# Loads of later chunks and of the check counted as landing later in the planner of a linear attention and MLP kernel

## The chip, the cores and the metric

The kernel runs on one core of a Trainium2 chip. The metric is device time in microseconds (us) of one execution. In the profile, PE is TensorE's matmul, PEld TensorE's weight load (which runs beside the matmuls), DVE is VectorE, ACT ScalarE, POOL GpSimd, SP SyncE, which here does nothing but issue DMAs.

## The reference

```python
# r, k, v, w: (4, 8, 768, 48); u: (8, 48)
for t in range(S):                                   # linear attention with decay
    kt, vt, rt, wt = (k[:, :, t], v[:, :, t], r[:, :, t], w[:, :, t])
    cur = np.einsum('bhd,bhe->bhde', u[None] * kt, vt)
    y[:, :, t] = np.einsum('bhd,bhde->bhe', rt, state + cur)
    state = wt[:, :, :, None] * state + np.einsum('bhd,bhe->bhde', kt, vt)
x = y.transpose(0, 2, 1, 3).reshape(3072, 384)
h = x @ w_in                                         # 384 -> 2048
g = np.maximum(h, 0.0) + alpha * np.minimum(h, 0.0)
out = g @ w_out                                      # 2048 -> 384
```

## The kernel before

**Chunks and groups.** The attention is cut into 24 chunks (q = 0 to 23) of 64 steps and two batches. Three chunks make a group of 384 tokens, and the eight groups go through the two matrix products of the MLP one after the other. A group's MLP is 16 units j, one for each 128 of the 2048 hidden features: `moe_up` (line 669: nine matmuls from x to a PSUM bank, in full and rest parts wh and wl), then the activation on ACT (line 674) and DVE (line 676), the split into gh (ACT, line 680) and its rest gl (DVE, line 681), and `moe_down` (line 694: three times three matmuls into op0, op1, op2). The products down of a unit follow those up by two units (`LAG`).

**A chunk's steps.** `load` issues its DMAs: wd (line 375), kr (line 376), rk (line 381, from chunk 5 on) and nv (line 382). `prep` works on them: two scans on DVE (lines 395 and 401) and two products into kr (lines 404 and 407), two products on POOL (line 425) that a reduction on DVE (line 428) makes cd of, and copies on ACT (line 433) into at. Then come a transpose of kr on PE (line 498) and a block of 128 small matmuls (line 452), which closes one chunk and opens the next; behind it stand x (ACT line 574, DVE line 585), the state St (DVE line 596) and the masked copies into at (line 483). When a group's third chunk is done, four small DMAs (line 606) move parts of x, and the group's units can begin. In each group from the third on, the second and the third chunk's blocks stand close together, about six microseconds apart; the text calls these two blocks a pair. There are pairs near 135, 193, 251, 311 and 371 us that other preparation follows.

**Weights and the check.** The 16 weight tiles are loaded (line 619) and unpacked on ACT (line 630) and DVE (lines 632, 635, 639: the product wf, one tile at a time), and split later into wh and wl (lines 650, 651). During the second half of the kernel, 12 pieces of wd and the 16 weight tiles are loaded a second time into two buffers raw (line 766) and tested on ACT (lines 774, 783, 784); the result is a flag that the end reads.

**What sets the order.** Nothing is ordered by hand. Every step is an `op` with an engine, a planned duration, a planned latency (`lat`) and a due time; `Plan.order` walks through a planned time and gives each free engine the ready step with the earliest due time. The instructions are then issued in that order, engine by engine, and on the chip every engine keeps to its order: an instruction whose input isn't there holds up all that stand behind it on its engine. For a load, the planned landing is in these lines:

```python
if e == "SP":
    dma = max(dma, end + DMA_LAT) + o.lat
    end = dma
```

with `DMA_LAT` 2.0 and 0.4 for the issue; the planned latencies are 1.5 for kr, 0.75 for wd and nv, 1.1 for rk and 2.0 for a piece of the check. `end` is when the steps that read the load become ready in the plan. The tiles come in rings: three for kr and nv, two for wd, rk and raw, so that the load of a chunk waits for the reader of the chunk two or three before it. Steps with `lock=True` on DVE and POOL aren't planned side by side.

## Time and profile before

| | |
|---|---|
| median of 3 runs | 511.61 us (507.61 to 512.86) |
| the profiled execution | 509.13 us, of which the profile's span is 507.3 us |
| PE busy, share of the span | 494.3 us, 97% |
| PEld busy | 457.8 us, 90% |
| DVE busy | 338.2 us, 67% |
| ACT busy | 290.8 us, 57% |
| mean granted clock of TensorE | 0.996 of full speed |

The profile is of one execution, which isn't one of the three runs. A matmul's row overlaps the next one's, so PE looks busy while it is short of work for a few tenths of a microsecond; the rows of PEld, one of which takes 0.19 us and which follow each other every 0.17 us when nothing is missing, show a wait at its full length.

### The profile page before, as it was taken

How to read it: one execution, taken by the hardware profiler on the slowest of the kernel's cores; microseconds unless marked ns; L12 is line 12 of the kernel's file. 1: busy time of each engine (PE TensorE's matmuls, PEld its weight loads, DVE VectorE, ACT ScalarE, POOL GpSimd, SP SyncE). 2: the span in 40 equal slices, each digit the busy share in tenths (PEclk: the TensorE clock that was granted, in tenths of full speed). 3: DMA queues.
4: the chain of work that ended last, by engine and by line, in shares of the span. 5: the costliest groups of instructions: out<-in, count | busy, mean ns of one | idle time of the engine just before them, and what ended most of it. 6: DMA issues, size and time to landing. Idle time of an engine off the chain costs nothing.

```text
span 507.3 us, 13038 instructions
## 1 busy us (share of the span) xinstructions
PE 494.3 (97%) x5404; PEld 457.8 (90%) x5404; DVE 338.2 (67%) x602; ACT 290.8 (57%) x746; POOL 79.4 (16%) x103
## 2 busy tenths in 40 slices
PE   8999998999999999999999999999999999999994
PEld 8976664699999999999998999989999999999994
DVE  7999999999886656938377474945566344343331
ACT  5866485453454536457584656667677676553331
POOL 2111333350114010402014020220000000000000
PEclk9999999999999999999999999999999999999998
DMA  8966776550352302735175653746455531210001
GB/s 311 365 212 228 265 238 213 151 161 23 111 149 79 112 22 77 221 90 202 49 216 163 159 175 105 237 131 205 147 179 159 170 127 63 88 42 6 1 3 53
DMA packets 27109, 72.42 MB, mean 143 GB/s; under 512 B 3680, under 2 KB 8224, under 8 KB 27040
## 3 DMA queue, kind: packets, MB, share of 16 engines
q1 hardware_dynamic: 26656, 71.19, 43.9%
q8 instruction: 44, 0.72, 0.6%
q10 hardware_dynamic: 384, 0.30, 0.2%
q14 instruction: 25, 0.20, 0.1%
HBM read 64.70 MB, written 4.72 MB: 137 GB/s over the span
## 4 chain that ended last, share of the span: by engine, by line
PE 78%; DVE 12%; DMA 5%; issue 2%; SPq 1%; ACT 1%; DVEq 0%; ACTq 0%
PE bank L669 35%; PE op L694 33%; PE bank L452 7%; DMA raw<-in_wts_dram 2%; DVE cx L635 2%; DVE wf L639 2%; DVE suf L395 2%; DMA kr<-in_dmaj_dram 1%; PE bank L498 1%; DVE pos L676 1%; DVE kr L404 1%; DVE kr L407 1%; DVE cx L632 1%; PE bank L561 1%; DVE wd L401 1%
## 5 line engine op out<-in xcount | busy, mean ns | idle before, releaser
L669 PE MATMUL bank<-x,wh 128*128 128x384 f32 x672 | 191.7, 339 | 0.5 <-DMA x<-x 0.5
L674 ACT ACTIVATE pos<-bank,alpha_n 128x384 f32<-128x384 f32 (+1 forms) x133 | 75.3, 567 | 100.7 <-PE bank L669 100.3
L676 DVE SCALAR_TENSOR_TENSOR pos<-bank,pos 128x384 f32<-128x384 f32 (+1 forms) x133 | 71.3, 536 | 82.3 <-ACT pos L674 82.1
L669 PEld LDWEIGHTS bank<-x,wh 128*128 128x128 f32 x672 | 123.0, 188 | 2.5 <-ACT os L711 1.1
L694 PE MATMUL op<-wh,gh 128*128 128x384 f32 x336 | 113.3, 337 | 0.8 <-ACT gh L680 0.8
L694 PE MATMUL op<-wh,gl 128*128 128x384 f32 x336 | 112.8, 336 | 1.4 <-DVE gl L681 1.2
L694 PE MATMUL op<-wl,gh 128*128 128x384 f32 x336 | 112.5, 335 | 0.0
L669 PE MATMUL bank<-x,wl 128*128 128x384 f32 x336 | 112.4, 335 | 0.0
L681 DVE TENSOR_TENSOR gl<-pos,gh 128x384 fp32r<-128x384 f32 x112 | 68.3, 610 | 55.6 <-ACT gh L680 54.9
L680 ACT CAST gh<-pos 128x384 fp32r<-128x384 f32 x112 | 57.4, 512 | 51.4 <-DVE pos L676 51.2
L694 PEld LDWEIGHTS op<-wh,gl 128*128 128x128 f32 x336 | 63.1, 188 | 2.5 <-DVE gl L681 2.5
L694 PEld LDWEIGHTS op<-wh,gh 128*128 128x128 f32 x336 | 63.1, 188 | 1.4 <-ACT gh L680 1.4
L669 PEld LDWEIGHTS bank<-x,wl 128*128 128x128 f32 x336 | 63.1, 188 | 0.1
L694 PEld LDWEIGHTS op<-wl,gh 128*128 128x128 f32 x336 | 63.1, 188 | 0.0
L443 POOL TENSOR_TENSOR St<-St,pc_all 128x192 f32<-128x192 f32 x44 | 25.1, 589 | 232.5 <-DVE St L596 172.1
L433 ACT ACTIVATE at<-twin,cd 128x64 f32<-128x64 f32 x192 | 52.9, 340 | 2.4 <-DVE cd L428 1.9
L425 POOL TENSOR_TENSOR rk<-rk,u_bc 128x384 f32<-128x384 f32 x19 | 24.3, 1279 | 93.2 <-DMA rk<-in_nat_dram 50.5
L669 PE MATMUL bank<-xw,wf 128*128 128x384 f32 (+2 forms) x126 | 35.3, 418 | 1.8 <-DVE wf L639 1.7
L694 PE MATMUL op<-wf,pos 128*128 128x384 f32 x96 | 34.4, 489 | 0.0
L395 DVE TENSOR_TENSOR_SCAN suf<-wd,low 128x528 f32<-128x528 f32 x24 | 30.0, 1248 | 3.7 <-DMA wd<-in_dmaj_dram 3.7
L669 PEld LDWEIGHTS bank<-xw,wf 128*128 128x128 f32 x126 | 20.6, 190 | 12.5 <-DVE wf L639 2.9
L401 DVE TENSOR_TENSOR_SCAN wd<-wd,low 128x528 f32<-128x528 f32 x24 | 31.6, 1318 | 0.1
(81 smaller groups left out, 530.5 us busy)
## 6 DMA issues: line engine op xcount, KB each, us to landing
raw<-in_wts_dram SPq DMA_DIRECT2D x32, 768.0 KB, 4.7
kr<-in_dmaj_dram SPq DMA_DIRECT2D x24, 512.0 KB, 4.0
rk<-in_nat_dram SPq DMA_DIRECT2D x19, 384.0 KB, 3.4
wd<-in_dmaj_dram SPq DMA_DIRECT2D x24, 264.0 KB, 2.9
raw<-in_dmaj_dram SPq DMA_DIRECT2D x12, 528.0 KB, 4.0
nv<-in_nat_dram SPq DMA_DIRECT2D x24, 256.0 KB, 4.9
out_dram<-os SPq DMA_DIRECT2D x44, 96.0 KB, 2.2
x<-x SPq DMA_DIRECT2D x28, 72.0 KB, 4.2
```

The costliest lines, as they stand in the source:

```text
L395: op("DVE", 1.17, lambda: nc.vector.tensor_tensor_scan(out=suf.ap[:, ::-1], data0=w.ap[:, ::-1], data1=low[:, ::-1], initial=0.0, op0=ALU. ...
L401: op("DVE", 1.17, lambda: nc.vector.tensor_tensor_scan(out=w.ap, data0=w.ap, data1=low, initial=0.0, op0=ALU.mult, op1=ALU.max), r=["low"] ...
L425: op("POOL", 1.0, lambda i=i: nc.gpsimd.tensor_tensor(out=rk.ap[:, 0:HD], in0=rk.ap[:, 0:HD], in1=u_bc if i == 0 else rk.ap[:, HD:], op=AL ...
L433: nc.scalar.activation(out=at.ap[:, o, p, :], in_=twin, func=AF.Copy, scale=cd.ap[:, o * NP + p:o * NP + p + 1])
L443: op("POOL", 0.6, lambda i=i: nc.gpsimd.tensor_tensor(out=St[b][:, i, :, 0:D], in0=St[b][:, i, :, 0:D], in1=pc_all[:, q, i::2].unsqueeze(2 ...
L452: nc.tensor.matmul(yb[q][i].ap[rows, cols], start=(i, rows.start) not in opened[q], stop=stop, skip_group_check=True, **kw)
L669: nc.tensor.matmul(hp.ap[:, ts], lhsT=a, rhs=b[:, k, ts], start=(i == 0), stop=(i == m - 1))
L674: op("ACT", 0.15 + 0.33 * share, lambda: nc.scalar.activation(out=pos.ap[:, ts], in_=hp.ap[:, ts], func=AF.Relu, scale=alpha_n[:, j:j + 1] ...
L676: op("DVE", 0.07 + 0.4 * share, lambda: nc.vector.scalar_tensor_tensor(out=pos.ap[:, ts], in0=hp.ap[:, ts], scalar=0.0, in1=pos.ap[:, ts], ...
L680: op("ACT", 0.43, lambda: nc.scalar.copy(out=gh.ap, in_=pos.ap), r=[pos], w=[gh])
L681: op("DVE", 0.47, lambda: nc.vector.tensor_tensor(out=gl.ap, in0=pos.ap, in1=gh.ap.bitcast(F32), op=ALU.subtract), r=[pos, gh], w=[gl], lo ...
L694: nc.tensor.matmul(ops_[s], lhsT=a.ap[:, ts], rhs=w, start=(j == 0 and i == 0), stop=(j == NF - 1 and i == len(todo) - 1))
```

## The change

Two numbers are new, `LATE` = 2.5 and `LATE_FROM` = 6. In the planner, a DMA step with a true `kind` is counted as landing 2.5 us later for the steps that read it; the planned time of the queue itself (`dma`) stays as it was. All loads of chunks 6 to 23 and the 28 loads of the check carry the mark; those of chunks 0 to 5, the first load of the weights, the moves of x and the stores don't. No instruction is added, removed or altered; only the order in which engines take them differs.

```diff
--- before.py
+++ after.py
@@ -58,6 +58,8 @@
 
 MODES = {("M", "Q"): 0.1, ("Q", "M"): 0.1}
 DMA_LAT = 2.0
+LATE = 2.5
+LATE_FROM = 6
 MADE = 12
 SPLIT = 0
 U_BY_PE = 5
@@ -202,7 +204,7 @@
                     lock = end
                 if e == "SP":
                     dma = max(dma, end + DMA_LAT) + o.lat
-                    end = dma
+                    end = dma + (LATE if o.kind else 0.0)
                 else:
                     end += o.lat + (0.15 if e == "PE" else 0.06)
                 heapq.heappush(ends, (end, o.n))
@@ -371,15 +373,15 @@
 
         def load(q):
             w, kr, rk, nv = (Tensor(r) for r in (r_w, r_kr, r_rk, r_nv))
-            natural = q >= U_BY_PE
-            op("SP", 0.4, lambda: nc.sync.dma_start(out=w.ap, in_=dmaj[q, :, 0:SC]), w=[w], lat=0.75)
+            natural, far = q >= U_BY_PE, q >= LATE_FROM
+            op("SP", 0.4, lambda: nc.sync.dma_start(out=w.ap, in_=dmaj[q, :, 0:SC]), w=[w], lat=0.75, kind=far)
             op("SP", 0.4, lambda: nc.sync.dma_start(out=kr.ap.rearrange("p i a t -> p (i a t)"), in_=dmaj[q, :, SC:DMC]),
-               w=[(kr, 0), (kr, 1)], lat=1.5)
+               w=[(kr, 0), (kr, 1)], lat=1.5, kind=far)
             if q == U_BY_PE:
-                op("SP", 0.4, lambda: nc.sync.dma_start(out=u_bc, in_=u.partition_broadcast(P)), w=["u"], lat=0.5)
+                op("SP", 0.4, lambda: nc.sync.dma_start(out=u_bc, in_=u.partition_broadcast(P)), w=["u"], lat=0.5, kind=far)
             if natural:
-                op("SP", 0.4, lambda: nc.sync.dma_start(out=rk.ap, in_=nat[q, :, 0:2 * HD]), w=[rk], lat=1.1)
-            op("SP", 0.4, lambda: nc.sync.dma_start(out=nv.ap, in_=nat[q, :, 2 * HD:2 * HD + VW]), w=[nv], lat=0.75)
+                op("SP", 0.4, lambda: nc.sync.dma_start(out=rk.ap, in_=nat[q, :, 0:2 * HD]), w=[rk], lat=1.1, kind=far)
+            op("SP", 0.4, lambda: nc.sync.dma_start(out=nv.ap, in_=nat[q, :, 2 * HD:2 * HD + VW]), w=[nv], lat=0.75, kind=far)
             loaded[q] = w, kr, rk, nv
 
         def prep(q):
@@ -763,7 +765,7 @@
         gap = (late - 20.0 - begin) / (NQ // 2 + NF)
 
         def check_load(i, src, out):
-            op("SP", 0.4, lambda: nc.sync.dma_start(out=out(), in_=src), w=[(raw, 0), (raw, 1)], lat=2.0, due=late,
+            op("SP", 0.4, lambda: nc.sync.dma_start(out=out(), in_=src), w=[(raw, 0), (raw, 1)], lat=2.0, kind=True, due=late,
                after=begin + i * gap)
 
         for i in range(NQ // 2):
```

What the planner makes of it begins at chunk 6. The first row that differs stands about 70 us into the kernel; from there on the orders of DVE and ACT differ in many places by one to a dozen rows, those of PE and POOL in few. In the changed file every line past 60 has a number two higher (L406 there is L404 here). Names with a number at the end (kr_2_120) are single buffers of a ring.

**Place 1: DVE at the third pair (near 257 us)**, which holds the preparation of two chunks: kr_1_119 is that of chunk 16, kr_2_120 that of chunk 17. Before, from the second chunk's x on:

```order
L585 TENSOR_TENSOR x_1_132<-bank_4_79,x_1_132 128x4x64
L585 TENSOR_TENSOR x_1_132<-bank_0_75,x_1_132 128x4x64
L596 TENSOR_TENSOR St0_109<-bank_4_79,St0_109 128x4x48
L596 TENSOR_TENSOR St0_109<-bank_0_75,St0_109 128x4x48
L483 COPY_PREDICATED at_1_130<-mask_100,bank_1_76 128x256
L676 SCALAR_TENSOR_TENSOR pos_2_137<-bank_2_77,pos_2_137 128x384
L483 COPY_PREDICATED at_1_130<-mask_100,bank_3_78 128x256
L398 RECIPROCAL low_97<-suf_0_126 128x8
L428 TENSOR_REDUCE cd_1_128<-rk_1_122 128x8
L681 TENSOR_TENSOR gl_2_143<-pos_2_137,gh_2_140 128x384
L401 SCALAR_TENSOR_TENSOR wd_1_117<-wd_1_117,low_97 128x528
L404 TENSOR_TENSOR kr_2_120<-kr_2_120,suf_0_126 128x512
```

After, from the product on chunk 16's kr on (x and St of that chunk stand ahead of it now):

```order
L406 TENSOR_TENSOR kr_1_119<-kr_1_119,suf_0_126 128x512
L409 TENSOR_TENSOR kr_1_119<-kr_1_119,wd_0_116 128x512
L485 COPY_PREDICATED at_1_130<-mask_100,bank_2_77 128x256
L485 COPY_PREDICATED at_1_130<-mask_100,bank_0_75 128x256
L397 SCALAR_TENSOR_TENSOR suf_0_126<-wd_1_117,low_97 128x528
L678 SCALAR_TENSOR_TENSOR pos_0_135<-bank_3_78,pos_0_135 128x384
L400 RECIPROCAL low_97<-suf_0_126 128x8
L430 TENSOR_REDUCE cd_0_127<-rk_0_121 128x8
L403 SCALAR_TENSOR_TENSOR wd_1_117<-wd_1_117,low_97 128x528
L683 TENSOR_TENSOR gl_0_141<-pos_0_135,gh_0_138 128x384
L678 SCALAR_TENSOR_TENSOR pos_1_136<-bank_4_79,pos_1_136 128x384
L406 TENSOR_TENSOR kr_2_120<-kr_2_120,suf_0_126 128x512
```

The first product on kr, its partner (L407) and the scan (L395) stood ahead of x before and stand behind x and St now; the product on the kr of chunk 17, which followed at once on the scan L401, has a gl and one more pos of the MLP between the scan and itself. At the pairs near 135, 193, 311 and 371 us the first chunk's three steps move behind x and St in the same way.

**Place 2: ACT near 328 us**, where the check of the weight tile in raw_1_114 begins. Before:

```order
L674 ACTIVATE pos_1_136<-bank_0_75,alpha_n_61 128x384
L784 ACTIVATE raw_0_113,wt_all_106<-raw_0_113,tiny_105 128x384
L680 CAST gh_1_139<-pos_1_136 128x384
L674 ACTIVATE pos_2_137<-bank_1_76,alpha_n_61 128x384
L410 COPY pc_all_107<-suf_0_126 128x8
L783 ACTIVATE raw_1_114<-raw_1_114 128x384
L680 CAST gh_2_140<-pos_2_137 128x384
L783 ACTIVATE raw_1_114<-raw_1_114 128x384
L784 ACTIVATE raw_1_114,wt_all_106<-raw_1_114,tiny_105 128x384
```

After:

```order
L676 ACTIVATE pos_1_136<-bank_4_79,alpha_n_61 128x384
L786 ACTIVATE raw_0_113,wt_all_106<-raw_0_113,tiny_105 128x384
L682 CAST gh_1_139<-pos_1_136 128x384
L676 ACTIVATE pos_2_137<-bank_0_75,alpha_n_61 128x384
L502 COPY kn_111<-bank_1_76 128x448
L682 CAST gh_2_140<-pos_2_137 128x384
L676 ACTIVATE pos_0_135<-bank_4_79,alpha_n_61 128x384
L412 COPY pc_all_107<-suf_0_126 128x8
L785 ACTIVATE raw_1_114<-raw_1_114 128x384 x2
L682 CAST gh_0_138<-pos_0_135 128x384
L786 ACTIVATE raw_1_114,wt_all_106<-raw_1_114,tiny_105 128x384 x2
```

The two squares of the check (L783, L785 after) stood ahead of the making of gh_2_140 and stand one unit later now, behind gh_2_140 and the next unit's first activation.

**Place 3: DVE near 80 us**, in the first group, where the weight tiles are unpacked (wf) beside chunk 6's preparation (kr_0_118). Before:

```order
L635 SCALAR_TENSOR_TENSOR cx_0_115<-raw_1_114,cx_0_115 128x768
L404 TENSOR_TENSOR kr_0_118<-kr_0_118,suf_0_126 128x512
L639 ISA wf13_94<-raw_1_114,cx_0_115 128x1536
L676 SCALAR_TENSOR_TENSOR pos_2_137<-bank_0_75,pos_2_137 128x384
L632 TENSOR_SCALAR cx_0_115<-raw_0_113 128x768
L407 TENSOR_TENSOR kr_0_118<-kr_0_118,wd_0_116 128x512
L635 SCALAR_TENSOR_TENSOR cx_0_115<-raw_0_113,cx_0_115 128x768
L651 TENSOR_TENSOR wl0_997<-wf0_81,wh_80 128x768
L639 ISA wf14_95<-raw_0_113,cx_0_115 128x1536
```

After:

```order
L641 ISA wf12_93<-raw_0_113,cx_0_115 128x1536
L406 TENSOR_TENSOR kr_0_118<-kr_0_118,suf_0_126 128x512
L634 TENSOR_SCALAR cx_0_115<-raw_1_114 128x768
L409 TENSOR_TENSOR kr_0_118<-kr_0_118,wd_0_116 128x512
L637 SCALAR_TENSOR_TENSOR cx_0_115<-raw_1_114,cx_0_115 128x768
L678 SCALAR_TENSOR_TENSOR pos_1_136<-bank_4_79,pos_1_136 128x384
L430 TENSOR_REDUCE cd_0_127<-rk_0_121 128x8
L641 ISA wf13_94<-raw_1_114,cx_0_115 128x1536
L678 SCALAR_TENSOR_TENSOR pos_2_137<-bank_0_75,pos_2_137 128x384
L634 TENSOR_SCALAR cx_0_115<-raw_0_113 128x768
L653 TENSOR_TENSOR wl0_989<-wf0_81,wh_80 128x768
L637 SCALAR_TENSOR_TENSOR cx_0_115<-raw_0_113,cx_0_115 128x768
```

Both products on chunk 6's kr stand ahead of wf13 now, where one stood before; two rows further on, behind a second part wl1, comes wf14.

## Rows read from the trace of the kernel before

**Rows 1.** The page's first part: busy time, share of the span and count.

```profile
PE 494.3 (97%) x5404; PEld 457.8 (90%) x5404; DVE 338.2 (67%) x602; ACT 290.8 (57%) x746; POOL 79.4 (16%) x103
```

**Rows 2.** Waits of all engines: line, releaser, us in total, times, longest.

```profile
ACT raw L783 <- DMA raw<-in_wts_dram: 6.3, 4, 3.3
...
DVE kr L404 <- DMA kr<-in_dmaj_dram: 2.6, 2, 2.2
```

**Rows 3.** Timeline, 259 to 274 us: start, duration, engine, line; idle before, releaser.

```profile
259.62 1.19 SPq L376 DMA_DIRECT2D kr<-in_dmaj_dram  x1
...
267.18 0.69 DVE L404 TENSOR_TENSOR kr<-kr,suf 128x512 f32<-128x512 f32 x1 [2.24 <-DMA kr<-in_dmaj_dram]
267.79 0.55 DVE L676 SCALAR_TENSOR_TENSOR pos<-bank,pos 128x384 f32<-128x384 f32 x1
...
268.94 0.19 PEld L694 LDWEIGHTS op<-wh,gh 128*128 128x128 f32 x1 [0.25 <-ACT gh L680]
...
270.02 0.53 DVE L681 TENSOR_TENSOR gl<-pos,gh 128x384 fp32r<-128x384 f32 x1
...
270.61 0.19 PEld L694 LDWEIGHTS op<-wh,gl 128*128 128x128 f32 x1 [1.49 <-DVE gl L681]
...
274.01 0.19 PEld L694 LDWEIGHTS op<-wh,gl 128*128 128x128 f32 x1 [0.32 <-DVE gl L681]
```

**Rows 4.** Timeline, 325 to 334 us.

```profile
325.08 0.56 ACT L674 ACTIVATE pos<-bank,alpha_n 128x384 f32<-128x384 f32 x1
...
325.15 0.44 SPq L766 DMA_DIRECT2D raw<-in_wts_dram  x1
...
327.91 0.58 ACT L674 ACTIVATE pos<-bank,alpha_n 128x384 f32<-128x384 f32 x1 [0.64 <-PE bank L669]
...
331.88 0.54 ACT L783 ACTIVATE raw<-raw 128x384 f32<-128x384 f32 x1 [3.30 <-DMA raw<-in_wts_dram]
...
332.88 0.19 PEld L694 LDWEIGHTS op<-wh,gh 128*128 128x128 f32 x1 [1.16 <-ACT gh L680]
333.47 0.19 PEld L694 LDWEIGHTS op<-wh,gl 128*128 128x128 f32 x1 [0.41 <-DVE gl L681]
```

**Rows 5.** The page's DMA issues: count, KB each, median us to landing.

```profile
kr<-in_dmaj_dram SPq DMA_DIRECT2D x24, 512.0 KB, 4.0
```

**Rows 6.** Timeline of the first group, 79 to 101 us.

```profile
79.19 1.48 DVE L404 TENSOR_TENSOR kr<-kr,suf 128x512 f32<-128x512 f32 x1
...
81.59 1.59 PEld L669 LDWEIGHTS bank<-xw,wf 128*128 128x128 f32 x6 [1.35 <-DVE wf L639]
...
87.35 1.59 PEld L669 LDWEIGHTS bank<-xw,wf 128*128 128x128 f32 x6 [1.59 <-DVE wf L639]
...
100.40 0.19 PEld L669 LDWEIGHTS bank<-x,wh 128*128 128x128 f32 x1 [1.11 <-ACT os L711]
```

**Rows 7.** Two pairs: the chain (start, us) and the timeline, 135 to 215 us.

```profile
135.63 2.02 PE bank L452 x128
...
137.39 0.63 DVE L596 TENSOR_TENSOR St<-bank,St 128x192 f32<-128x192 f32 x2 [0.41 <-ACT x L574]
...
199.29 2.02 PE bank L452 x128
...
199.80 0.69 DVE L404 TENSOR_TENSOR kr<-kr,suf 128x512 f32<-128x512 f32 x1
...
204.65 0.51 DVE L428 TENSOR_REDUCE cd<-rk 128x8 f32<-128x384 f32 x1
...
207.18 0.69 DVE L404 TENSOR_TENSOR kr<-kr,suf 128x512 f32<-128x512 f32 x1 [0.36 <-DMA kr<-in_dmaj_dram]
...
211.78 1.84 POOL L425 TENSOR_TENSOR rk<-rk 128x384 f32<-128x384 f32 x1
...
212.74 1.31 DVE L681 TENSOR_TENSOR gl<-pos,gh 128x384 fp32r<-128x384 f32 x1
...
214.10 0.19 PEld L694 LDWEIGHTS op<-wh,gl 128*128 128x128 f32 x1 [0.24 <-DVE gl L681]
```

## The prediction, made before the run

> **What bounds the kernel now.** I read the page's busy shares first: PE is at 97% and its weight loads at 90% of the span, DVE at 67% [rows 1]. So the kernel is matmul-bound, and an instruction moved on another engine counts only where PE waits for it; no instruction is added or taken away, so PE's own work stays the same. Next come the waits, where the change is about loads. Two kinds of instruction on the compute engines waited for a load that the change marks: the first product on kr on DVE, twice and 2.6 us in all, and the squares of the check on ACT, four times and 6.3 us [rows 2]. Then the timeline, to see which of these reached PE. Two did.
>
> The first is near 267 us [rows 3]. The load of chunk 17's kr was issued at 259.62 and the product on it began at 267.18, after 2.24 us of waiting: 7.5 us from issue, where the median kr load takes 4.0 [rows 5]. Behind the product stood pos of a unit of the MLP (267.79), on which gh and gl (270.02) rest, and the weight loads of PE show three holes, of 0.25, 1.49 and 0.32 us. The second is near 332 us [rows 4]. A piece of the check was issued at 325.15 and its square ran at 331.88, after 3.30 us of idle ACT; gh, which the squares stood ahead of, came late, and PE shows holes of 1.16 and 0.41 us. Outside these two, from 101 us on, PE has one more hole by a late operand of the MLP, 0.24 us at 214 [rows 7]. Before 101 us there are three that matter, 1.35, 1.59 and 1.11 us [rows 6]; they are the unpacking of weights on DVE and the move of x.
>
> **The change part by part.** All sums are made against the profiled execution, 509.13 us, which is 2.5 us below the median of 511.61.
>
> *First hole.* The planner counted on 0.4 + 2.0 + 1.5 = 3.9 us for the kr load, and now counts on 6.4. In the new order (place 1) chunk 16's two products and scan go behind x and St, and one pos more comes ahead of chunk 17's product. As worked out below for the pairs, DVE begins these steps 1.25 us later than before; the pos is 0.55 us [rows 3]. So the product moves 1.8 us towards the landing, and 0.4 of the 2.24 us of waiting may stay. (PE's block of this pair stands a unit later as well, but the load waits for that block's reading of the old kr, so load and product move together.) gl now stands ahead of the product. What is late next is nothing on PE, as this kr is first read there by the transposes of chunk 17, about a dozen units on. Of the 0.25 + 1.49 + 0.32 = 2.1 us of holes I take 1.8 off, the share of the wait that goes; the bounds are 0 (a load still later) and 2.1.
>
> *Second hole.* The check's squares go one unit down (place 2), behind the gh that PE waited for and the next unit's activation. Activations of units stand 2.8 us apart [rows 4], so the squares come at about 328.6 + 2.8 = 331.4, against a landing at 331.9; and what would wait there then is the next unit's gh, which isn't due yet. I take off 1.16 + 0.41 = 1.6 us; the bounds are 0 and 1.6.
>
> *First group* (place 3). Chunk 6's second product on kr moves ahead of wf13, and it is 0.6 us long, or 1.5 when a POOL instruction runs beside it, as its partner at 79.19 shows (1.48 against 0.69 [rows 6, 7]). PE already waits 1.35 us for wf13, so this hole grows by 0.6 to 1.4. wf14, 1.59 us late, has the same steps ahead of it but for one part wl more and that product one place earlier; so most of the growth comes off the next hole. What ends the group is the move of x, for which PE waits 1.11 us, and up to x's last copy DVE does the same steps in either order. So I count 0, between -1.6 (the product of 82 us now runs without POOL, and so does a step behind it) and +0.9.
>
> *The pairs.* Here the order costs something. At four pairs (135 to 311 us) DVE did the first chunk's two products and scan while PE ran the block and gave it nothing to do; now they stand behind St. At the pair of 199 us, DVE was free of gl at 199.80 and PE's block began at 199.29. St comes 1.76 us after a block begins (135.63 to 137.39), so at 201.05. The gap of 1.25 us takes the reduction cd of 0.51, which the new order puts there; 0.74 us are idle in which DVE worked before, and the wait of 0.36 us for kr at 207.18 goes away [rows 7]. DVE is then some 0.4 us later with the last gl of this stretch. That gl was already late by 0.24 us, since it took 1.31 us beside a POOL product at 211.78 in place of 0.53 [rows 3, 7]. If POOL meets it again, PE loses 0.4 us more, and 0.8 on top if POOL meets a product on kr too: 1.2. If POOL's products fall elsewhere, it loses nothing. Between 0 and 1.2 I take 0.3 a pair, nearest to the row with the one collision, and 1.2 for four; the bounds are 0 and 5.0. The pair near 371 us has no third chunk to prepare and costs nothing.
>
> The sum: 509.13 - 1.8 - 1.6 + 0 + 1.2 = 506.9 for an execution like the profiled one. The median execution is 2.5 us slower. If it is so by more such waits, these go too, and 506.9 holds for it; if by something else, it is 511.61 - 2.2 = 509.4. No row tells the two apart, so I forecast between them, **508.2 us**, 0.7% below the median.
>
> A rule speaks against the first step. The row shows 7.5 us for a load of 512 KB, against a median of 4.0. The Trainium skill (DMA: Bandwidth & Descriptors, section Anatomy of one DMA) gives a DMA about 2.0 us fixed and its bytes by 436 GB/s, fitted on the GpSimd path: an estimate of 3.2 us here. By that rule the planner's 3.9 was already enough, the first two terms would be 0 and the sum 510.3. The trace doesn't agree, since even its median is above.
>
> **The rivals.** *The late loads were accidents of this execution.* Most kr loads land as the plan had it (median 4.0 [rows 5]), and 2.5 us more for all of them moves work behind a load that is there. If the median execution has no such holes, nothing is gained and the pairs cost 1.2: 512.8 us. Against it speaks that two of the ten or so exposed places in one execution were hit, so others will be in others. This is also what the skill's rule would make of it.
>
> *Everything above the best is load waits.* Then both terms are had in every execution, the pairs cost nothing, and the median comes to 509.13 - 3.7 = 505.4 or, with the first group's lower bound, 503.8. For it speaks that the runs differ by 5 us with the same instructions and that the marked loads of chunks have a spread; against it, that the first group waits for weight loads, too, which the change doesn't mark.
>
> *Slower: DVE becomes late at the pairs.* The burst behind the block meets POOL's two products each time. It decides from 0.9 us a pair on, where four pairs eat the 3.4 us; at their bound they give 509.13 - 3.4 + 5.0 = 510.7 for the profiled kind of execution and 513.2 for the median; without the gain, and with the front's 0.9, 511.61 + 5.0 + 0.9 = 517.5. For it: the gl at 212.74, late already. Against it: the planner keeps such steps of DVE and POOL apart, and it now counts the POOL's inputs (rk) as later, which is nearer to the chip. The Trainium skill (SBUF — State Buffer, section SBUF: two separate sides) has it that DVE with two SBUF inputs and GpSimd lock each other out for a whole instruction. By that rule, the trace agrees: 1.31 and 1.48 us beside POOL against 0.53 and 0.69.
>
> **How the numbers follow.** The forecast has 0.5 (506.5 to 510.5), everything as load waits 0.25, accidents 0.15, slower pairs 0.1. A range from 505.0 to 512.8 leaves out about the lower half of the second case and the tail of the last. A measurement of this kernel tells 1% (5.1 us) from no change, about as much as its runs differ. Faster by over 1% needs less than 506.5: the second case and a little of the first, 0.28. Slower by over 1%, above 516.7, needs the last one at its bound: 0.04. Within 1%: 0.68.
>
> **What would show it.** Right: near 267 and 332 us no hole of PE's weight loads above 0.3 us, no kr product on DVE that waits for its load, squares on ACT that wait under 1 us. PE's holes before 101 us still some 4 us, with the one at wf13 longer. At the pairs gl a little later, holes of 0 to 0.5 us by gl. Wrong: holes by gl of over 0.9 us at several pairs, a wait for x of over 1.5 us at the end of the first group, or new waits for kr and raw at other places.

## The result, and the profile after

The changed kernel takes 511.98 us (median of 22 runs, 510.38 to 517.87) against 511.11 us before, measured beside it (22 runs, 506.42 to 514.63). The ratio is 1.008, 95% interval 1.0056 to 1.0104; it is taken over the fast runs of each kernel (those within 1.5% of its fastest), the medians over all of them, which are only 0.9 us apart. The lowest runs are 4.0 us apart. The forecast was 508.2 us, 0.7% faster. By the ratio it is slower by 0.8%; the time lies inside the range given, the sign is the other one. The profiled execution of the changed kernel took 510.84 us, its span 509.0.

The page's first part shows the same instruction counts as [rows 1], but DVE and POOL are busier, DVE by 7.5 us and POOL by 4.0:

```profile
PE 496.4 (98%) x5404; PEld 458.5 (90%) x5404; DVE 345.7 (68%) x602; ACT 290.2 (57%) x746; POOL 83.4 (16%) x103
```

The waits of the changed kernel, to set beside [rows 2] (line, releaser, us in total, times, longest). The two waits of [rows 2] are gone: no row for the squares on raw (L785 now) and none for the first product on kr (L406 now). In their place the row of PE's weight loads that wait for gl has grown from four times and 2.5 us to eleven times (before, then after):

```profile
PEld op L694 <- DVE gl L681: 2.5, 4, 1.5
```

```profile
PEld op L696 <- DVE gl L683: 4.7, 11, 0.6
```

The two places of the forecast, in the timeline. Chunk 17's kr, late in [rows 3], is issued at 263.79; its product runs at 273.44 and waits for nothing. The check's squares of [rows 4] run at 335.09 without a wait:

```profile
263.79 0.72 SPq L378 DMA_DIRECT2D kr<-in_dmaj_dram  x1
...
273.44 0.68 DVE L406 TENSOR_TENSOR kr<-kr,suf 128x512 f32<-128x512 f32 x1
...
335.09 1.00 ACT L785 ACTIVATE raw<-raw 128x384 f32<-128x384 f32 x2
```

So both holes that the change was to close are closed: 2.06 and 1.57 us. What came instead is best seen near 180 us, behind a block that stands alone, where a third chunk's preparation moved by a unit. Before, the two products on kr ran at 175.32, as soon as DVE was free; POOL's products met one gl (1.40 us) and PE lost nothing:

```profile
175.32 0.68 DVE L404 TENSOR_TENSOR kr<-kr,suf 128x512 f32<-128x512 f32 x1
175.92 0.68 DVE L407 TENSOR_TENSOR kr<-kr,wd 128x512 f32<-128x512 f32 x1
...
178.78 1.01 POOL L425 TENSOR_TENSOR rk<-rk 128x384 f32<-128x384 f32 x1
178.80 1.40 DVE L681 TENSOR_TENSOR gl<-pos,gh 128x384 fp32r<-128x384 f32 x1 [0.47 <-ACT gh L680]
```

After, DVE idles 1.76 us there, and the products run behind the next pos. POOL's first product now runs beside the second one (1.50 in place of 0.68) and its second one beside gl (1.36 in place of 0.53), one behind the other, and PE waits 0.61 us:

```profile
179.29 0.56 DVE L678 SCALAR_TENSOR_TENSOR pos<-bank,pos 128x384 f32<-128x384 f32 x1 [1.76 <-ACT pos L676]
179.76 0.68 DVE L406 TENSOR_TENSOR kr<-kr,suf 128x512 f32<-128x512 f32 x1
180.02 1.29 POOL L427 TENSOR_TENSOR rk<-rk,u_bc 128x384 f32<-128x384 f32 x1 [5.95 <-DMA rk<-in_nat_dram]
180.36 1.50 DVE L409 TENSOR_TENSOR kr<-kr,wd 128x512 f32<-128x512 f32 x1
181.39 1.35 POOL L427 TENSOR_TENSOR rk<-rk 128x384 f32<-128x384 f32 x1
181.79 1.36 DVE L683 TENSOR_TENSOR gl<-pos,gh 128x384 fp32r<-128x384 f32 x1
...
183.21 0.19 PEld L696 LDWEIGHTS op<-wh,gl 128*128 128x128 f32 x1 [0.61 <-DVE gl L683]
```

The same rows, with 0.61 us each, come again near 242 and 301 us. Behind single blocks the holes by gl are 0.38, 0.61, 0.61, 0.61 and 0.37 us, 2.58 in all; behind pairs 0.20, 0.53, 0.27, 0.47, 0.43 and 0.17, 2.07 in all. In six of the eleven gl itself is stretched (1.30 us or more). In the other five (0.38, 0.20, 0.27, 0.37 and 0.43) it has its usual 0.53 or 0.54 us and is late by steps stretched further up, up to 5 us before, as DVE doesn't idle in between.

What is new is not that gl meets POOL: it takes over 0.7 us nine times in the trace of the kernel before and eight times in that of the changed one. New are the second products on kr. From 92 to 433 us not one of them was stretched in the kernel before, and eight of them are in the changed one, seven beside POOL's products on rk and one, near 267 us, beside one on the state (count; min, median and max in ns; before, then after):

```profile
L407 DVE TENSOR_TENSOR kr<-kr,wd x17: 677/683/686, 101.3 to 384.7; 128x512 f32<-128x512 f32 x17
```

```profile
L409 DVE TENSOR_TENSOR kr<-kr,wd x17: 675/685/1504, 102.7 to 389.0; 128x512 f32<-128x512 f32 x17
```

In the first group, to set beside [rows 6], the hole at wf13 is 1.03 us, in front of it stands a new one of 1.39 by pos, and the one at wf14 is nearly gone. The hole in front of the block near 71 us, which waits for a masked copy into at, is 1.44 us in place of 0.75:

```profile
71.72 0.32 PEld L454 LDWEIGHTS bank<-kr,St 64*64 64x64 f32 x16 [1.44 <-DVE at L485]
...
83.17 0.30 PEld L696 LDWEIGHTS op<-wf,pos 128*128 128x128 f32 x2 [1.39 <-DVE pos L678]
84.49 1.59 PEld L671 LDWEIGHTS bank<-xw,wf 128*128 128x128 f32 x6 [1.03 <-DVE wf L641]
88.91 1.04 PEld L671 LDWEIGHTS bank<-xw,wf 128*128 128x128 f32 x4 [0.24 <-DVE wf L641]
...
101.99 0.19 PEld L671 LDWEIGHTS bank<-x,wh 128*128 128x128 f32 x1 [1.03 <-ACT os L713]
```

**Two yardsticks.** Times of whole executions spread by 8 us with one order in the 22 runs above, and by 11 us in the 121 named below. Two things make single traces comparable. The first is the distance between weight loads of the same block: from the block near 51 us to the one near 92 us is the first group with what leads up to it, from there to the block near 433 us is nearly all the rest; what happens before 50 us stays out. The second is TensorE's clock: of 121 runs of the kernel before, 53 have a mean granted clock below 0.994, and their median is 511.4 to 512.5 us in each of the four series that the experiments were measured in; the other 68 have one of 507.7 us (506.6 to 507.9 by series). In the profiled executions of the low kind (not_kr, zero_nopool, kr17, dve12_marks and dve_after) the lower clock lies between 18 and 30 us, and in dve_after once more from 105 to 111 us; here that of not_kr (columns: window, length, PE busy, granted clock, DMA share, GB/s):

```profile
10.00:16.00 6.00, 5.88 (x130) 1.00 1.02 388
18.00:27.00 9.00, 9.00 (x84) 0.50 0.71 272
30.00:40.00 10.00, 10.00 (x170) 1.00 0.59 189
```

From 18 to 27 us the clock is granted at 0.50, the 1.2 GHz level, and before and behind at 1.00. The order up to there is that of before in each of the kernels, so this is no effect of the change. In the tables, "full clock" is the median of the runs at 0.994 or more.

Of the changed kernel's 22 runs, 15 are at full clock, with a median of 511.2 us, 3.5 above the 507.7 of the other series.

### The profile page after: what moved, and what is told of

Read it like the earlier page. It is cut to its first block, busy times and chain, and to the rows that moved or that the text cites. A ratio compares the mean times of both kernels' runs of the same rounds, so it can differ in the third digit from the quotient of the medians.

```text
span 509.0 us, 13046 instructions
## 1 busy us (share of the span) xinstructions
PE 496.4 (98%) x5404; PEld 458.5 (90%) x5404; DVE 345.7 (68%) x602; ACT 290.2 (57%) x746; POOL 83.4 (16%) x103
## 4 chain that ended last, share of the span: by engine, by line
PE 78%; DVE 12%; issue 3%; DMA 2%; ACT 2%; SPq 0%; POOL 0%; DVEq 0%; ACTq 0%; POOLq 0%
PE bank L671 34%; PE op L696 32%; PE bank L454 8%; DVE wf L641 2%; DMA raw<-in_wts_dram 2%; DVE gl L683 2%; DVE cx L637 2%; PE bank L500 1%; DVE suf L397 1%; PE bank L725 1%; DVE cx L634 1%; DVE kr L406 1%; PE op L820 1%; DVE pos L678 1%; PE bank L563 1%
## 5 line engine op out<-in xcount | busy, mean ns | idle before, releaser
L427 POOL TENSOR_TENSOR rk<-rk,u_bc 128x384 f32<-128x384 f32 x19 | 28.6, 1503 | 72.6 <-DMA rk<-in_nat_dram 60.8
L397 DVE TENSOR_TENSOR_SCAN suf<-wd,low 128x528 f32<-128x528 f32 x24 | 34.3, 1429 | 3.9 <-DMA wd<-in_dmaj_dram 3.9
```

The lines of the kernel that those rows point to most:

```text
L397: op("DVE", 1.17, lambda: nc.vector.tensor_tensor_scan(out=suf.ap[:, ::-1], data0=w.ap[:, ::-1], data1=low[:, ::-1], initial=0.0, op0=ALU. ...
L427: op("POOL", 1.0, lambda i=i: nc.gpsimd.tensor_tensor(out=rk.ap[:, 0:HD], in0=rk.ap[:, 0:HD], in1=u_bc if i == 0 else rk.ap[:, HD:], op=AL ...
```

## The experiments

**Theory 1** says that the marks of the loads move the preparation of chunks into the front of gl, which costs in every execution, while of the two load waits not both do. **Theory 2**: the cost lies before 110 us. **Theory 3**: the check's marks carry it. Later, 1a and 1b ask which loads' marks do it, C and D by which means: C by DVE and POOL meeting, D by the moved steps' own length. All kernels are edits of the changed file; ratios and differences are against the kernel before, measured in the same series.

| kernel | marks | ratio (95%) | full clock, against before, us | holes by gl, us (times) |
|---|---|---|---|---|
| before, changed | none; all | -; 1.008 (1.0056 to 1.0104) | - | 2.5 (4); 4.7 (11) |
| zero | none | 1.0002 (0.9966 to 1.0038) | +1.1 | 2.4 (4) |
| loads_only | chunks 6 to 23 | 1.0112 (1.0047 to 1.0177) | +5.5 | 5.4 (9) |
| check_only | check | 1.0012 (0.997 to 1.0055) | +1.7 | 1.8 (2) |
| from9 | chunks 9 to 23, check | 1.0063 (1.0024 to 1.0103) | +3.5 | 3.6 (8) |
| kr_only | kr of chunks 6 to 23 | 1.0052 (1.0017 to 1.0088) | +1.1 | 3.1 (6) |
| not_kr | wd, rk, nv of 6 to 23 | 1.0036 (0.9997 to 1.0075) | +1.3 | 3.0 (6) |
| after_nopool | all | 0.996 (0.9925 to 0.9994) | -4.5 | 0 |
| zero_nopool | none | 0.9958 (0.9914 to 1.0002) | -4.7 | 1.5 (1) |
| kr17 | kr of chunk 17 | 0.9984 (0.9946 to 1.0022) | -0.5 | 0.6 (2) |
| pool14 | all | 1.012 (1.0068 to 1.0172) | +4.9 | 5.4 (10) |
| dve_after | all | 1.0049 (1.0007 to 1.009) | +2.5 | 0.2 (1) |
| dve_zero | none | 1.0117 (1.0062 to 1.0172) | +4.1 | 2.2 (5) |
| first_group | chunks 6 to 8 | 1.0013 (0.9978 to 1.0048) | +0.5 | 2.4 (5) |
| dve9_marks | as from9 | 0.9937 (0.9902 to 0.9973) | -1.4 | 0 |
| dve9_nomarks | none | 0.9999 (0.9963 to 1.0034) | -0.6 | 1.5 (1) |
| dve12_marks | chunks 12 to 23, check | 0.9931 (0.9891 to 0.9972) | -2.7 | 1.9 (2) |

The medians at full clock rest on 3 to 9 runs; that of zero, the order of before, comes out 1.1 us off, so differences of that size say nothing. Three single executions, of 699 us (before), 990 (dve9_marks) and 2791 (dve_after), are left out. The distances between the blocks, from the traces:

| kernel | block at 51 to 92, us | block at 92 to 433, us |
|---|---|---|
| before | 41.98 | 341.49 |
| zero | 40.80 | 340.20 |
| changed | 42.14 | 341.96 |
| loads_only | 42.12 | 343.48 |
| check_only | 40.91 | 339.36 |
| from9 | 40.87 | 341.21 |
| kr_only | 40.81 | 340.70 |
| not_kr | 42.10 | 341.31 |
| first_group | 42.10 | 340.58 |
| pool14 | 42.85 | 344.44 |
| dve_after | 40.24 | 344.36 |
| dve_zero | 40.22 | 343.75 |
| zero_nopool | 39.39 | 339.23 |
| after_nopool | 39.40 | 336.97 |
| kr17 | 41.21 | 338.22 |
| dve12_marks | 42.03 | 339.46 |
| dve9_nomarks | 41.69 | 339.44 |
| dve9_marks | 43.17 | 337.78 |

Two traces of one order, before and zero, differ by 1.2 us in the first column and by 1.3 in the second.

### Which marks

zero:

```diff
-LATE = 2.5
+LATE = 0.0
```

> The changed file with LATE = 0.0, which gives the order of the kernel before (line numbers as in the changed file). It leaves nothing out. Theory 1 (the loads' marks move the preparation of chunks next to gl, and gl is late 11 times, 4.65 us in all, in every execution, while the load waits near 267 and 332 us fall in some executions only): ratio 0.997 to 1.003, lowest run 506.4 to 508, and in another trace of this order the holes near 267 and 332 us are smaller or elsewhere, gl holes under 1 us in all. Theory 2 (the cost lies before 110 us: the hole of 1.16 us at 17 us and the first group): the same time, the hole at 17 us 0.3 or less here. On the spread: if it is TensorE's clock, the runs above 511 show a granted clock under 0.994 and those below 509 over 0.995; if it is load waits, the clock is the same in both.

The ratio is that of no change; the lowest run, 505.41 us, lies below the 506.4 that was expected. The wait of the product on chunk 17's kr is there again, and the load takes 7.5 us again, so it is no accident of one execution, against theory 1, which had it in some executions only (and under 1 us by gl, where 2.4 came). The long wait of the check's squares isn't (2.0 at most, in place of 3.3):

```profile
ACT raw L785 <- DMA raw<-in_wts_dram: 6.0, 5, 2.0
PEld op L696 <- DVE gl L683: 2.4, 4, 1.5
DVE kr L406 <- DMA kr<-in_dmaj_dram: 2.2, 1, 2.2
```

```profile
260.10 0.81 SPq L378 DMA_DIRECT2D kr<-in_dmaj_dram  x1
...
267.60 0.69 DVE L406 TENSOR_TENSOR kr<-kr,suf 128x512 f32<-128x512 f32 x1 [2.17 <-DMA kr<-in_dmaj_dram]
...
271.03 0.19 PEld L696 LDWEIGHTS op<-wh,gl 128*128 128x128 f32 x1 [1.48 <-DVE gl L683]
```

Of its own runs, the three above 509.4 us have clocks of 0.987 to 0.990, the nine others 0.995 or more: mostly the clock sets the spread, as one reading of the expectation had it. Its bound of 511 us was too high.

loads_only and check_only take one kind of mark each:

```diff
-... lat=2.0, kind=True, due=late,      # loads_only: the check unmarked
+... lat=2.0, due=late,
-LATE_FROM = 6                          # check_only
+LATE_FROM = 24
```

> Only the loads of chunks 6 to 23 are marked, the check's are not. Theory 1: all of the cost, ratio 1.006 to 1.010, lowest run about 510, and holes by gl of PE's weight loads of about 4.5 us in all (11 or so holes), at the same steps as in the changed kernel. Theory 2: the same ratio, but from holes before 110 us. Theory 3 (the check's marks on ACT's order carry the cost): ratio 0.997 to 1.001, holes by gl under 1.5 us.

> LATE_FROM = 24, so only the loads of the check are marked. Theory 1: none of the cost, ratio 0.995 to 1.001, lowest run 505.5 to 507.5, holes by gl under 1.5 us, no hole by the squares of the check near 332 us. Theory 2: ratio 1.000, the front as before. Theory 3: ratio 1.006 or more, with holes behind ACT's steps between 280 and 450 us.

The loads' marks alone cost all of it (1.0112), the check's alone nothing that the ratio tells (1.0012). Theory 3 falls. loads_only has its holes by gl near the steps of the changed kernel for the most part, and a larger one, of 1.12 us near 281 us. Without the check's marks the part from 92 us on is 1.5 us longer, hardly more than two traces of one order differ. check_only has no hole by the squares near 332 us, as theory 1 had it, but two by gl at other places, 1.83 us in all, where under 1.5 was expected.

from9 and first_group split the loads' marks by place:

```diff
-LATE_FROM = 6
+LATE_FROM = 9                                  # from9
-natural, far = q >= U_BY_PE, q >= LATE_FROM
+natural, far = q >= U_BY_PE, 6 <= q < 9        # first_group, check unmarked
```

> LATE_FROM = 9: the loads of chunks 6, 7 and 8 are not marked, so the first group has the order of before; all later marks stay. Theory 1: only the gl hole of 0.38 us at 128 us goes, ratio 1.004 to 1.009, lowest run about 510. Theory 2: ratio 0.998 to 1.003, lowest run 506.5 to 508, with the holes before 110 us as in the kernel before (4.8 us from 68 to 101 us).

> Only the loads of chunks 6, 7 and 8 are marked. If the first group carries about a quarter of the loss (theory 1, from the run that leaves these marks out): ratio 1.001 to 1.004, holes of 1.4, 1.4 and 1.0 us near 71, 82 and 84 us, later ones as in the order of before with that at 269 us. If it carries most of it (theory 2): 1.006 to 1.010.

Up to the block near 92 us nine traces have the order of before (before, zero, check_only, from9, kr_only, kr17, dve9_marks, dve9_nomarks and dve12_marks): 40.80 to 43.17 us, with a median of 41.21. Four have that of the changed kernel (changed, loads_only, not_kr, first_group): 42.10 to 42.14. The rows of from9, and behind them those of the changed kernel:

```profile
50.92 0.33 PEld L454 LDWEIGHTS bank<-kr,St 64*64 64x64 f32 x16 [0.55 <-issue]
...
91.79 0.32 PEld L454 LDWEIGHTS bank<-kr,St 64*64 64x64 f32 x16 [0.55 <-issue]
```

```profile
51.34 0.33 PEld L454 LDWEIGHTS bank<-kr,St 64*64 64x64 f32 x16 [0.55 <-issue]
...
93.48 0.32 PEld L454 LDWEIGHTS bank<-kr,St 64*64 64x64 f32 x16 [0.55 <-issue]
```

So the first group carries about 0.9 us, less than single executions of one order differ there (up to 2.4). Theory 2 in its strong form falls, since without these marks the ratio is still 1.0063, and with them alone 1.0013.

kr_only and not_kr split them by load:

```diff
-... lat=0.75, kind=far)      # wd and nv; rk with lat=1.1 as well: kr_only
+... lat=0.75)
-... lat=1.5, kind=far)       # kr: not_kr
+... lat=1.5)
```

> Only the loads of kr of chunks 6 to 23 are marked (not wd, rk, nv, nor the check's). Theory 1a (kr's mark carries the cost: it moves a chunk's two products on kr by a unit, into the front of gl): ratio 1.004 to 1.011, holes by gl of 3 us or more in all, among them those of 0.6 us at about 182, 241 and 301 us. Theory 1b (the marks of wd, rk and nv carry it, by the scans and by the time at which POOL's products start): ratio 0.995 to 1.002, holes by gl under 1.5 us outside of the order of before.

> The other half: wd, rk and nv of chunks 6 to 23 are marked, kr and the check are not. Theory 1a: ratio 0.999 to 1.004, of which the first group may have 1 us, holes by gl as in the order of before (about 2.5 us with those near 270). Theory 1b: ratio 1.005 or more.

Both ratios lie where 1a had them (1.0052, and 1.0036, whose interval just reaches 1), but the intervals overlap and the full-clock medians, +1.1 and +1.3, don't part the two: that kr's mark costs more than the others isn't shown. The traces part them by the means. The repeated 0.62 us at 181 and 240 us comes with kr's mark, as 1a had it, though not the third of them near 301 us; six second products on kr are stretched in kr_only, none in not_kr. The other order of the first group comes with the other marks, and not_kr has holes that 1a hadn't, of 0.75 and 0.48 us, where gl stands beside POOL at 187 and 221 us. Either kind of move makes new meetings; both together (loads_only) have more holes by gl than either.

### By which means

after_nopool and zero_nopool keep each order and leave out POOL's two products:

```diff
-op("POOL", 1.0, lambda i=i: nc.gpsimd.tensor_tensor(
-    out=rk.ap[:, 0:HD], in0=rk.ap[:, 0:HD], in1=u_bc if i == 0 else rk.ap[:, HD:], op=ALU.mult),
+op("POOL", 1.0, lambda i=i:
+    None,
```

> The changed kernel in its order, with the two products on POOL of chunks 5 to 23 left out (so the bonus term is wrong; cd reduces the loaded rk); every other instruction stands where it stood. To be compared with zero_nopool. Theory C (gl is late since POOL's products stretch the DVE steps ahead of it and gl itself): the two come within 1.5 us of each other in runs of the same clock, and holes by gl are under 1.5 us in all. Theory D (the steps moved ahead of gl make it late by their own length, with POOL or without): this one stays 3 us or more slower than zero_nopool, with holes by gl of 3 us or more.

> The order of the kernel before with the same two products on POOL left out. Theory C: POOL costs this order little, ratio 0.995 to 1.000, and after_nopool is within 1.5 us. Theory D: the same ratio, with after_nopool 3 us or more above. In both the hole near 269 us by kr of chunk 17 stays (about 2 us).

This decides between C and D. With POOL's products away the two orders take the same time (503.2 and 503.0 us at full clock, five runs each), where D had 3 us or more between them, and not one weight load waits for gl in the changed order. DVE's busy time falls from 345.7 to 327.5 us in the changed order and from 338.7 to 326.3 in the other: by that difference POOL's products lengthen DVE's work by 18.2 us in the one and 12.4 in the other. That DVE waits for POOL's results is no rival, since no step on DVE has such a wait in the traces of before, zero and the changed kernel. At the place near 180 us (175 here) the moved products and gl stand in the same row and take 0.68, 0.68 and 0.55 us:

```profile
174.93 0.56 DVE L678 SCALAR_TENSOR_TENSOR pos<-bank,pos 128x384 f32<-128x384 f32 x1 [1.82 <-ACT pos L676]
175.40 0.68 DVE L406 TENSOR_TENSOR kr<-kr,suf 128x512 f32<-128x512 f32 x1
176.00 0.68 DVE L409 TENSOR_TENSOR kr<-kr,wd 128x512 f32<-128x512 f32 x1
176.61 0.55 DVE L683 TENSOR_TENSOR gl<-pos,gh 128x384 fp32r<-128x384 f32 x1
```

From 92 to 433 us the changed order is even 2.3 us shorter in these traces than the order of before, which has the holes at chunk 17's kr; with POOL it is 0.5 to 1.8 us longer. The medians don't show these 2.3 us. The blocks' rows, after_nopool and then zero_nopool:

```profile
90.32 0.33 PEld L454 LDWEIGHTS bank<-kr,St 64*64 64x64 f32 x16 [0.55 <-issue]
...
427.29 0.32 PEld L454 LDWEIGHTS bank<-kr,St 64*64 64x64 f32 x16 [0.25 <-DVE pos L678]
```

```profile
95.28 0.32 PEld L454 LDWEIGHTS bank<-kr,St 64*64 64x64 f32 x16 [0.55 <-issue]
...
434.51 0.32 PEld L454 LDWEIGHTS bank<-kr,St 64*64 64x64 f32 x16 [0.25 <-DVE pos L678]
```

D falls: without POOL beside them the moved steps' own length makes no hole by gl.

pool14 lets the planner count POOL's products longer; dve_after and dve_zero put them on DVE:

```diff
-op("POOL", 1.0, lambda i=i: nc.gpsimd.tensor_tensor(
+op("POOL", 1.4, lambda i=i: nc.gpsimd.tensor_tensor(     # pool14
+op("DVE", 0.47, lambda i=i: nc.vector.tensor_tensor(     # dve_after, dve_zero
```

> The changed kernel with all marks and the two products on POOL, which the planner counts as 1.4 us each in place of 1.0 (on the chip they take 1.0 alone and 1.3 to 1.8 beside DVE). Theory C: fewer gl beside POOL, holes by gl under 3 us, ratio 1.000 to 1.006, below the changed kernel's 1.008. Theory D: as the changed kernel, 1.006 to 1.010.

> The changed kernel with all marks, but the two products of rk run on DVE instead of POOL (0.47 us each in the plan); nothing is left out. Theory C (the loss comes from DVE and POOL meeting): no stretched gl, so holes by gl under 1.5 us in all and a ratio of 0.993 to 0.999, within 1.5 us of dve_zero in runs of the same clock. Theory D (moved steps cost by their own length): 1.003 or more, since DVE gets 20 us more of work, and 3 us above dve_zero.

> The order of plan of before (LATE = 0.0) with the two products of rk on DVE instead of POOL. Theory C: ratio 0.993 to 0.999, DVE busy up by about 8 us on 338.7 (20 more by its own products, 12 less by the steps that POOL no longer stretches), holes of load waits as before. Theory D: ratio 1.000 to 1.004, DVE late with gl at several chunks.

All three came out slower than C forecast. pool14 has as many meetings as the changed kernel (nine products on kr and eight gl stretched, against eight and eight), the 1.37 us of gl and the 0.62 us of PE at 186, 245 and 304 us among them. On the chip POOL mostly starts when rk lands, which another planned duration doesn't set: in the changed kernel's trace 16 of the 19 first products waited for that landing. pool14's order also differs in the first group, with a hole of 2.43 us by wf. dve_after has the holes that C named (0.2 us, one), but loses 3.9 us behind 102 us, where PE waits for the move of x, and 0.7 twice by pos up to 130 us; during the 3.9 us the clock fell to 0.50, where it stayed until about 111 us. dve_zero loses 2.8 us behind 99 us and 0.7 twice by pos. The four moves of x took a median of 2.7 us from issue to landing in zero, 4.7 in dve_zero and 5.8 in dve_after, although dve_zero issued them at the time of zero (96.5 and 96.3 us); why isn't shown. So by its ratio dve_after fits D as well, but not by its holes. The waits for pos fit a DVE that is full there (busy for 38.0 of the 38 us from 92 to 130 us in zero). dve_zero also has the wait of the check's squares again (2.9 us).

### A version that beats both

kr17 marks one load. dve9_marks and dve12_marks put the products on DVE from chunk 9 or 12 on alone, with marks from the same chunk on; dve9_nomarks has LATE = 0.0.

```diff
-... lat=1.5, kind=far)           # kr17: kr alone, wd, rk, nv and the check unmarked
+... lat=1.5, kind=q == 17)
-op("POOL", 1.0, lambda i=i: nc.gpsimd.tensor_tensor(
+op(*(("DVE", 0.47) if q > 8 else ("POOL", 1.0)), lambda i=i: (nc.vector if q > 8 else nc.gpsimd).tensor_tensor(
-LATE_FROM = 6
+LATE_FROM = 9
```

> Only one load is marked, that of chunk 17's kr, which took 7.5 us from issue in both traces of the order of before. Theory 1a with collisions: the hole of 2.0 us near 269 us goes and no other preparation moves, ratio 0.994 to 0.999. Rival (the wait only moves to the next late step): ratio 1.000 to 1.003, with a hole of 1 us or more by gl or gh between 255 and 285 us. The rest leaves nothing out.

> Marks from chunk 9 on and on the check; the two products of rk run on DVE from chunk 9 on, on POOL before; nothing is left out. Theory C (the meeting of DVE and POOL is the loss): holes by gl under 0.8 us in all from 130 us on, no load wait near 269 and 332 us, the holes before 101 us as before: ratio 0.988 to 0.997, lowest run under 504.5. Theory D (more or later work on DVE makes gl late by its length): ratio 1.000 to 1.006.

> The same with LATE = 0.0. Theory C: the load wait at chunk 17 (2 us) and a few of gl stay, ratio 0.994 to 1.000, about 2 us above dve9_marks in runs of the same clock. Theory D: ratio 1.000 to 1.004, and below dve9_marks.

> As dve9_marks, from chunk 12 on for both, so that the splitting of the weights (to 130 us) is over. Theory C: ratio 0.988 to 0.996; better than dve9_marks where that one has DVE late before 140 us. Theory D: 1.000 to 1.006.

kr17 loses the hole near 269 us (the part from 92 us on is 2.0 us shorter than in zero), but its ratio, 0.9984, can't be told from 1. dve9_marks and dve12_marks are faster than the kernel before, at 0.9937 and 0.9931 with intervals below 1. Their medians over all runs are 506.7 us, against 510.0 before; but only 2 of 11 and 4 of 12 of their runs were at the lower clock, against 18 of 35 before, and at full clock they gain 1.4 and 2.7 us, the first hardly more than what zero was off. dve9_marks has no wait of the kr product or of the squares for a load, as expected; its lowest run, 505.1 us, misses the bound of 504.5. The 1.9 us of holes by gl in dve12_marks are a new load wait: the product on kr near 154 us waits 2.7 us for its load. In dve9_marks no weight load waits for gl, and the row that cost 0.61 us in the changed kernel stands there in the same order with nothing beside it:

```profile
179.78 0.68 DVE L406 TENSOR_TENSOR kr<-kr,suf 128x512 f32<-128x512 f32 x1
180.38 0.69 DVE L409 TENSOR_TENSOR kr<-kr,wd 128x512 f32<-128x512 f32 x1
180.98 0.56 DVE L683 TENSOR_TENSOR gl<-pos,gh 128x384 fp32r<-128x384 f32 x1
```

How much of this gain the marks have isn't settled. By the ratios it is 0.6%, but dve9_nomarks had 7 of its 12 runs at the lower clock and dve9_marks 2 of 11; at full clock they differ by 0.8 us, where 2 were expected. From 92 us on, where their orders part, the traces give the marks 1.7 us; the 1.5 us that dve9_marks is longer before it are chance, since the order there is the same.

## Why the prediction was wrong

**First hole: right.** The wait for chunk 17's kr returned in zero, and with the marks both are gone, the wait and all 2.06 us of holes (1.8 foretold). The rule of the Trainium skill that spoke against it (DMA: Bandwidth & Descriptors, section Anatomy of one DMA; an estimate of 3.2 us for such a load) is off by more than a factor of two here; 7.5 us was measured in both traces of the order. That the hole's end shortens the median by as much isn't shown: kr17, which ends it alone, gains 0.5 us at full clock.

**Second hole: right in the trace, but not to be had each time.** The squares no longer wait. zero shows that the 1.57 us weren't in every execution of the order of before, so the median gains less than the profiled execution.

**First group: at its upper bound.** 0 was taken, between -1.6 and +0.9. Against the profiled execution (41.98 us) it was +0.16, against the median of the nine traces of its order (41.21) +0.9. The profiled execution had a slow first group by chance, so most of the price was hidden in the base. The text also left out the hole in front of the block near 69 us (0.75 us by a masked copy into at), which grew to 1.44.

**The pairs: the step that failed.** The text counted the cost of moved preparation at four pairs, at 0.3 us each, and nowhere else. The pairs cost 0.5 each (2.07 in all, of which 0.24 stood there before). The single blocks, between the pairs, weren't in the sum, and cost 2.58 us more. There too a chunk's two products on kr move by a unit, and what makes them dear is not that they are late but that the second of them comes to stand beside POOL's products, in a row with a scan or a gl that is stretched too: eight such products take 0.78 to 1.50 us in place of 0.68, 3.9 us more in all, where none was stretched before. The mechanism stood among the rivals, as DVE late beside POOL, with the right price for one meeting (1.36 and 1.50 us in the trace, 1.31 and 1.48 foretold) and with the wrong places: it needed no 0.9 us a pair, since it had eight places, four pairs and four single blocks. The argument against it, that the planner keeps such steps apart, was wrong as well. The planner does it in its own time; on the chip POOL mostly starts when rk lands. The Trainium skill (Perfetto Trace Analysis, section Optimizing Scalar/DVE Operations) warns that moving work between DVE and GpSimd may not help, since they share a read port to SBUF. The traces agree that the two hold each other up: the same product takes 1.0 to 2.9 us on POOL and stretches a DVE step beside it by up to 0.8, and takes 0.55 on DVE. As to the help, both came: moving all of the products cost time (dve_after, 1.0049), moving those from chunk 9 on, with the marks, gained some (0.9937).

**The base.** The text couldn't tell what made the median 2.5 us slower than the profiled execution, and took half of it as load waits. The later series point to the clock of the first 30 us: full-clock runs of the order of before have a median of 507.7 us, less than the profiled 509.13, and those at the low clock one of 511.4 to 512.5. The profiled execution was a slow one of its kind, by the second hole and the first group. The three runs of the forecast's base have no clock on record; by their times, one or two at the low clock probably set their median. With what was measured, the sum is 507.7 + 0.9 (first group) + 4.65 - 0.24 (gl) - 2.06 (first hole) = 510.95 us, where the full-clock runs of the changed kernel have 511.2. So close a meeting is partly luck, as full-clock medians of one order lie between 506.6 and 507.9. The distances say the same more roughly: against zero, the changed kernel's trace is 1.3 us longer in the first group and 1.8 from there on, 3.1 of the 3.5 us.

What the text named as signs came out in part: the two holes gone, no wait for kr, no wait of the squares, as foretold; no single hole by gl above 0.9 us, but eleven of up to 0.61. PE's holes before 101 us were still some 4 us, but the one at wf13 got shorter (1.03 us in place of 1.35), with the new one in front of it.

## What to carry to other kernels

A planner that counts a load as later doesn't only avoid a wait; it moves all that hangs on the load, and each moved step has new neighbours on the other engines. So count the places from the order, all of them, and ask at each what runs beside the step at its new time. Before pricing against a profiled execution, see from a second trace of the same order which of its holes come back, and take its time as the base only when it is near the middle of the runs.

## What the hardware showed beyond that

DVE and POOL lengthen each other, and what PE pays depends on what DVE has ahead. Before, a gl of 1.40 us beside a POOL product, behind 0.47 us of idle DVE, cost PE nothing, and one of 1.31 behind a busy DVE cost 0.24 us at 214 us [rows 7]; after, a product of 1.50 and a gl of 1.36 behind it cost 0.61 us. Over all 112 instructions gl (min, median and max in ns) was never above 560 ns where POOL's products were away; first the changed kernel, which has them, then dve9_marks:

```profile
L683 DVE TENSOR_TENSOR gl<-pos,gh x112: 525/559/1369, 105.9 to 499.2; 128x384 fp32r<-128x384 f32 x112
```

```profile
L683 DVE TENSOR_TENSOR gl<-pos,gh x112: 531/558/560, 106.5 to 495.4; 128x384 fp32r<-128x384 f32 x112
```

A mean granted clock below 0.994 came in 53 of 121 executions of one program, and cost 3.6 to 4.8 us by series. In all five traces of this kind the clock fell behind 18 us, and PE had stood still for 0.9 to 1.8 us shortly before (in not_kr for about 1.0 us, up to 17.65). But traces that kept the full clock have such a standstill as well, the changed kernel's one of 1.16 us at the same place and kr_only one of 1.49:

```profile
18.00:27.00 9.00, 8.96 (x164) 1.00 0.82 298
```

What decides between the two wasn't tried.
